# Blocked attention and a gated feed-forward layer on one core: two tiles turned by TensorE instead of by DMA, one product moved, wider products of zeros

## The chip, the cores and the metric

The kernel runs on one core of a Trainium2 chip, in one launch. The metric is the device time of that core in microseconds. A profile of one execution on the chip lies beside the times; its span runs from the first to the last instruction.

## What is computed

Attention within sorted blocks, then a feed-forward layer. `sort_net` is balanced five times (a softmax along rows, then a division along columns) into a matrix P that mixes the eight blocks of k and v; each block of 96 queries attends to its mixed block; the result, laid out by token, goes through `w_in`, `h * cos(h)` and `w_out`:

```python
P = balanced(sort_net)                       # 4 x 8 heads, 8 x 8 blocks, five rounds
k_sorted = einsum('bhij,bhjcd->bhicd', P, k_blocks)
v_sorted = einsum('bhij,bhjcd->bhicd', P, v_blocks)
scores = scale * q_block @ k_sorted_block.T  # 96 x 96 for each block
attn = exp(scores - max); attn = attn / sum(attn)
x = (attn @ v_sorted_block) by token         # 3072 x 512
h = x @ w_in                                 # 512 -> 2048
out = (h * cos(h)) @ w_out                   # 2048 -> 512
```

## The kernel before

The 3072 tokens are worked in eight chunks of 384, numbered n = 0 to 7. A chunk is four token tiles u = 0 to 3 of 96 rows, all eight heads in each. For a tile, `qk(n, u)` (line 490; `qk_half` at 495 does half the heads) makes the scores on TensorE and takes the row maximum off on VectorE; `expo(n, u)` (501) takes the exponential on ScalarE into one of three buffers `p_buf` and has it turned into the tile `pT` (or a piece of `vperm` from chunk 5 on), since the next product needs it turned. The turning goes one of two ways. By default SP issues a DMA transpose (519). With `on_pe`, `p_transpose` (528) does it later: eight TensorE products against the identity into a PSUM tile `pps`, and a copy on the engine that it is given. `av(n, u)` (535) multiplies with the sorted v and divides by the row sum on VectorE, into `xn`; `xn` too must be turned, into `xT[n]`, and again either by a DMA transpose from SP (560) or, with `on_pe`, by `x_transpose` (564): four TensorE products into `xps` and a copy.

The feed-forward layer of a chunk is `moe_up` (633), eight pairs of `up` with the cosine on ScalarE and the product on VectorE, and `moe_down` (638), six groups of `down` (604): group e is half e % 2 of output tile e // 2, eight products of 512 columns each, which add up in one bank of the PSUM pool `acc`. `acc` has two banks, `big` three tiles of two banks. Attention of chunk n + 1 is laid between the groups of chunk n.

The order of all work is written out by hand (`tc.manual_schedule()`, line 67), and each engine works its own queue in that order. Lists of calls stand behind the pieces of `moe_up` and `moe_down`: `slots[e]` runs behind group e, and `mid` inside a group, between its fourth and fifth product. Before the change `mid` is a list that belongs to the last group (line 642). `down` steps through it at line 613.

SP's queue carries the DMA transposes, in the order in which the calls stand, and the stores. GpSimd's queue carries the loads of q, k, v and the weights (line 134 loads a chunk's queries), copies such as `v_permute` (167), and `hold` (521) or `p_hold` (525): a copy of one column that makes GpSimd wait until a tile is there before it goes on.

`keep_warm(times)` (216) issues products of zeros into a tile `idle` of `big` that nobody reads. It is called ahead of the balancing (223), after its first products `sk` (271), and in round 0 of the loop of line 329 (343, three times in that round, none in the others). In each round of the loop ScalarE takes the exponential `E` (331), TensorE sums along the columns (`sk`, 262) and VectorE divides (350, 324, 326), for two groups of batches; the products that turn the first queries (`qps`, 301) stand among them.

The steps of the prediction are these: lines 816 to 834, chunk 1's output with chunk 2's attention; 880 to 882, chunk 4's output with the attention of chunk 5; 895 to 897, chunk 6's output with that of chunk 7.

Of the kernel before, what the change touches and what calls it, by code (L numbers as in the profile page):

```python
# [10 lines left out]
FP32 = mybir.dt.float32  # L11
# [7 lines left out]
def kernel(  # L19
# [15 lines left out]
    nc = tc.nc  # L35
    B, H, S, D = q.shape
# [13 lines left out]
    TC = IC * blk  # L50
# [13 lines left out]
    big = ctx.enter_context(tc.tile_pool(name="big", bufs=3, space=bass.MemoryType.PSUM))  # L64
# [51 lines left out]
    def where(n):  # L116
        b, ih = n // 2, n % 2
        return b // 2, b % 2, ih
# [26 lines left out]
    def q_transpose_dma(n):  # L145
        for e in range(2):
            nc.sync.dma_start_transpose(
                out=q_of(n, e)[:, :QW].rearrange("p (x c) -> p x c", c=blk),
                in_=q_zeroed(n)[:, e * QZ:(e + 1) * QZ])
# [58 lines left out]
    warm = const.tile([128, 128], BF16, name="warm")  # L208
# [6 lines left out]

    def keep_warm(times):

        idle = big.tile([128, 256], FP32, name="idle", tag="big")
        for _ in range(times):
            nc.tensor.matmul(  # L220
                idle[:], warm[:], warm[:, :1].to_broadcast([128, 256]), start=True, stop=True)

    keep_warm(16)


    E_eps = [const.tile([128, nb + 1], FP32, name=f"E{g}") for g in range(NG)]
# [33 lines left out]
    def product(lhs, rhs):  # L260
        ps = acc.tile([128, nb], FP32, name="sk", tag="acc")
        nc.tensor.matmul(  # L262
            ps[:], lhs.rearrange("p x j -> p (x j)"), rhs, start=True, stop=True)
        return ps

    for g in range(NG):
        nc.vector.reciprocal(ci[g][:], cs[g][:])
        nc.vector.scalar_tensor_tensor(
            L[g][:], rows_of, ci[g][:], along(E[g]), op0=ALU.mult, op1=ALU.mult)
    sk = [product(L[g], maskj[:]) for g in range(NG)]  # L270
    keep_warm(3)
    nc.vector.tensor_copy(same[:], rows_of)
    nc.vector.tensor_copy(
        maskp.rearrange("p (b e x) -> p b e x", b=2, e=2),
# [11 lines left out]
    def copy_on(eng, dst, src):  # L286
        if eng is nc.scalar:
            eng.copy(dst, src)  # L288
        else:
            eng.tensor_copy(dst, src)  # L290

    V, A = nc.vector, nc.scalar
# [100 lines left out]
    def k_sort_g(t0, eng, pool, tag):  # L393
        ps = pool.tile([128, 4, 4 * NB], FP32, name="ks", tag=tag)
        for t in range(4):
            k_products(ps, t, t0 + t, slice(0, 128), bds[1].rearrange("p x i -> p (x i)"),
                       pair)
        copy_on(
            eng, kT2[:, ::2, :, :, t0:t0 + 4].rearrange("p e b m t -> p b e m t"),
            ps.rearrange("p t (b e m) -> p b e m t", b=2, e=2))  # L400
# [64 lines left out]
    def v_at(g, b2, hp, h2, i):  # L465
        return (b2 * 2 + hp) * NB + h2 * nb + i
# [34 lines left out]
    def expo(n, u, on_pe=False):  # L501
        p = p_bufs[cnt[0] % NP]
        cnt[0] += 1


        nc.scalar.activation(  # L506
            p[:, :, :blk], s_t.pop((n, u)).rearrange("p e h c -> p (e h) c"), AF.Exp,
            scale=scale)
        if n < LATE:
            t = ptp.tile([128, 2 * H2, blk], BF16, name="pT", tag="pT")  # L510
        else:

            z, w = (n * IC + u) % 8, 2 * H2 * blk
            t = vperm[:, z * w:(z + 1) * w].rearrange("p (a c) -> p a c", c=blk)
        pT[n, u] = t
        if on_pe:
            pb[n, u] = p
        else:
            nc.sync.dma_start_transpose(out=t[:], in_=p.rearrange("p a c -> p (a c)"))

    def hold(t):

        nc.gpsimd.tensor_copy(held[:blk], t[:blk, 0, :1])

    def p_hold(n, u):
        hold(pT[n, u])

    def p_transpose(n, u, eng, pool, tag):
        p = pb.pop((n, u))
        ps = pool.tile([128, 2 * H2, 128], BF16, name="pps", tag=tag)  # L530
        for a in range(2 * H2):
            nc.tensor.transpose(ps[:blk, a, :blk], p[:, a, :blk], ident[:blk, :blk])  # L532
        copy_on(eng, pT[n, u][:blk], ps[:blk, :, :blk])

    def av(n, u, on_pe=False):
        g, b2, ih = where(n)
        if n not in xT:
            xT[n] = xtp.tile([128, KC, TC], BF16, name="xT", tag="xT")
        a = big.tile([128, 2, 512], FP32, name="av", tag="big")
        pt = pT.pop((n, u)).rearrange("p a c -> p (a c)")  # L540
        for hp in range(2):
            for h2 in range(H2):
                e = hp * H2 + h2
                w = 128 if e < 2 * H2 - 1 else blk
                nc.tensor.matmul(  # L545
                    a[:w, hp, h2 * (D + 1):(h2 + 1) * (D + 1)],
                    pt[:blk, e * blk:e * blk + w],
                    vS[g][:, v_at(g, b2, hp, h2, ih * IC + u), :D + 1],
                    start=True, stop=True)
        avv = a[:blk, :, :H2 * (D + 1)].rearrange("p e (h w) -> p e h w", w=D + 1)  # L550
        r = small.tile([blk, 2, H2], FP32, name="r", tag="r")
        nc.vector.reciprocal(r[:].unsqueeze(3), avv[:, :, :, D:])  # L552
        xn = small.tile([blk, H2, 2, D], BF16, name="xn", tag="xn")
        nc.vector.tensor_tensor(  # L554
            xn.rearrange("p h e d -> p e h d"), avv[:, :, :, :D],
            r.to_broadcast([blk, 2, H2, D]), op=ALU.mult)
        if on_pe:
            xn_t[n, u] = xn
        else:
            nc.sync.dma_start_transpose(  # L560
                out=xT[n][:, :, u * blk:(u + 1) * blk],
                in_=xn.rearrange("p h e d -> p (h e d)"))
# [34 lines left out]
    def store(n, ts, o_s, eng=nc.sync):  # L597
        r0 = n * TC + ts * 128
        eng.dma_start(out=out[r0:r0 + 128, :], in_=o_s[:])
# [4 lines left out]
    def down(n, ts, half, stores, mid=()):  # L604
        if half == 0:
            out_ps[ts] = acc.tile([128, Dm], FP32, name="o", tag="acc")
        o = out_ps[ts]
        for f in range(half * FC // 2, (half + 1) * FC // 2):
            nc.tensor.matmul(  # L609
                o[:], gt[n, f // 2][:, f % 2, ts * 128:(ts + 1) * 128], w_out_t[:, f, :],  # L610
                start=(f == 0), stop=(f == FC - 1))
            if f % (FC // 2) == FC // 4 - 1:
                step(mid)
        if half == 0:
            return
        if stores is None:

            z = (n % 2 * 3 + ts) * 2 * Dm
            o_s = vbuf[:, z:z + 2 * Dm].bitcast(FP32)
        else:  # L620
            o_s = op.tile([128, Dm], FP32, name="o_s", tag="o_s")
        late = n > 0 and ts == TC // 128 - 1
        copy_on(V if late else A, o_s[:], o[:])
        if stores is None:
            kept[n, ts] = o_s
        else:
            store(n, ts, o_s, nc.sync if late else stores)

    def step(calls):
        for f, *args in calls:  # L630
            f(*args)
# [3 lines left out]
            up(n, fp, lo, hi)  # L635
            step(slots[fp] if fp < len(slots) else ())

    def moe_down(n, slots=(), stores=nc.sync, mid=()):

        last = 2 * TC // 128 - 1  # L640
        for e in range(last + 1):
            down(n, e // 2, e % 2, stores, mid if e == last else ())
            step(slots[e] if e < len(slots) else ())

    B, C = (big, "big"), (acc, "acc")
# [174 lines left out]
    k_sort_g(8, A, *B)  # L820
    av(2, 0, True)
    k_sort_g(16, A, *B)
    expo(2, 3)
    p_hold(2, 3)
    down(1, 1, 1, nc.sync)
    k_sort_g(12, A, *B)
    av(2, 2, True)
    av(2, 1, True)
    down(1, 2, 0, nc.sync)
    x_transpose(2, 1, V, *B)  # L830
    av(2, 3, True)
# [9 lines left out]
    def ahead(n, *more):  # L841
# [5 lines left out]
        for e, calls in more:  # L847
# [5 lines left out]
    moe_down(2, ahead(3, (0, [(ones, 1)]),  # L853
                      (1, [(w_two,)]), (2, [(p_hold, 3, 3), (load_q, 5), (w_two,)]),
                      (3, [(w_two,)]), (4, [(w_two,)])),
             mid=[(x_transpose, 3, 1, V, *B), (x_transpose, 3, 2, V, *B),
                  (x_transpose, 3, 3, V, *B)])
    q_transpose_dma(5)
    hold(q_turned[1])
    load_q(6)  # L860
# [7 lines left out]
                 [(av, 4, 0)],  # L868
                 [(av, 4, 1, True), (av, 4, 2, True)],
                 [(av, 4, 3, True), (expo, 5, 0), (x_transpose, 4, 1, A, *B, 2), (qk, 5, 1)]],  # L870
             None, mid=[(x_transpose, 4, 3, A, *B)])

    q_transpose_dma(6)
    hold(q_turned[0])
# [2 lines left out]
               [(qk_half, 5, 2, 1)], [], [(qk, 5, 3)]])  # L877
    expo(5, 1)
    expo(5, 2)
    moe_down(4, [[(qk, 6, 0)], [(av, 5, 0), (expo, 5, 3)], [(av, 5, 1), (qk, 6, 1)],  # L880
                 [(av, 5, 2), (expo, 6, 0)], [(av, 5, 3, True), (expo, 6, 1), (qk, 6, 2)]],
             None, mid=[(x_transpose, 5, 3, A, *B)])
    q_transpose_dma(7)
    moe_up(5, [[], [], [(qk_half, 6, 3, 0), (let_go, 4, 0)], [(let_go, 4, 1)], [(let_go, 4, 2)],
               [(qk_half, 6, 3, 1)], [], [(qk, 7, 0)]])
# [1 line left out]
    expo(6, 3)  # L887
    moe_down(5, [[(av, 6, 0)], [(av, 6, 1)], [(av, 6, 2), (qk, 7, 1)],
                 [(av, 6, 3, True), (expo, 7, 0)], [(expo, 7, 1), (qk, 7, 2)]], None,
             mid=[(x_transpose, 6, 3, A, *B)])  # L890
    moe_up(6, [[(let_go, 5, 0)], [(let_go, 5, 1)], [(qk_half, 7, 3, 0), (let_go, 5, 2)], [], [],
               [(qk_half, 7, 3, 1)]])
    expo(7, 2)
    expo(7, 3)
    moe_down(6, [[(av, 7, 0)], [(av, 7, 1)], [(av, 7, 2)], [(av, 7, 3, True)]], None,
             mid=[(x_transpose, 7, 3, A, *B)])
    moe_up(7, [[(let_go, 6, 0)], [(let_go, 6, 1)], [(let_go, 6, 2)]])
    for e in range(2 * TC // 128 - 2):
        down(7, e // 2, e % 2, nc.sync)
# [43 lines left out]
```

## Time and profile before

| What | Value |
|---|---|
| Median of three runs | 245.31 us (244.78 to 245.96) |
| The profiled execution | 245.54 us |
| Its span | 243.8 us |
| Mean granted TensorE clock | 0.949 |
| HBM read, written | 27.27 MB, 6.29 MB |

PE is TensorE's products, PEld its loading of weights, DVE VectorE, ACT ScalarE, POOL GpSimd, SP the queue of SyncE; "SPq" and "POOLq" are the issuing of a transfer. A timeline row reads: start in us, duration in us, engine, line, operation, what is written from what, shape, count, and in brackets how long the engine stood idle ahead of it and what ended that. A row of the chain that ended last reads: start, duration, what. A row of windows reads: from and to, length, busy time of PE, PEld, DVE, ACT and POOL with counts, granted clock (1.00 is full), share of the DMA engines, GB/s. A row of transfers gives the us from issue to landing at its end; a group's row has the shortest, middle and longest duration in ns.

### The profile page before, as it was taken

What the parts mean: (1) busy time and instruction counts of PE and PEld (TensorE: products, weight loads), DVE (VectorE), ACT (ScalarE), POOL (GpSimd) and SP (SyncE); (2) the same over time, 40 slices, a digit from 0 to 9 for tenths busy, and PEclk for the clock granted to TensorE, in tenths of its full rate; (3) what the DMA queues carried; (4) which work ended last, traced back from release to release, by engine and by line L of the source; (5) the groups of instructions that cost most, each with busy time, mean ns of one, the idle gap of its engine ahead of it and who ended that gap; (6) DMA issues with size and microseconds to landing.
All of it is one profiled execution on the core that took longest, in us unless ns stands there. A gap on an engine that the chain in (4) does not pass through costs nothing.

```text
span 243.8 us, 5363 instructions
## 1 busy us (share of the span) xinstructions
PE 230.7 (95%) x2160; PEld 148.4 (61%) x2160; DVE 173.6 (71%) x320; ACT 156.2 (64%) x224; POOL 88.0 (36%) x110
## 2 busy tenths in 40 slices
PE   7979899799999989999999999997999999999994
PEld 5768788565566546656666565654565566446553
DVE  5569678986579955895768987896789769635700
ACT  4468866576488945888569947683568376736611
POOL 6359994099970899010626201700000000000000
PEclk9655599999999999999999999999999999999999
DMA  4999999991999987865789759925581360233012
GB/s 46 231 192 161 184 206 227 198 218 52 166 164 183 162 137 94 128 159 146 120 110 129 77 122 157 182 52 85 117 222 33 89 191 0 53 70 122 1 46 86
DMA packets 67897, 31.20 MB, mean 128 GB/s; under 512 B 56608, under 2 KB 63392, under 8 KB 67616
## 3 DMA queue, kind: packets, MB, share of 16 engines
q0 software_dynamic: 24048, 13.64, 40.6%
q1 hardware_dynamic: 43312, 17.02, 31.2%
q8 instruction: 17, 0.28, 0.5%
q10 hardware_dynamic: 512, 0.20, 0.3%
q14 instruction: 8, 0.07, 0.1%
HBM read 27.27 MB, written 6.29 MB: 138 GB/s over the span
## 4 chain that ended last, share of the span: by engine, by line
PE 77%; DVE 7%; ACT 7%; DMA 6%; issue 1%; ACTq 0%; SPq 0%; DVEq 0%
PE h L585 32%; PE o L609 27%; PE sc L427 3%; PE av L545 3%; PE ks L360 2%; DVE gg L592 2%; PE vs L450 2%; DMA vperm<-p_buf 2%; DMA pT<-p_buf 2%; PE vs L460 2%; DVE xn L554 1%; PE pps L532 1%; PE xps L572 1%; ACT p_buf L506 1%; PE sk L262 1%
## 5 line engine op out<-in xcount | busy, mean ns | idle before, releaser
L585 PE MATMUL h<-xT,w_in_t 128*128 128x384 bf16 (+1 forms) x576 | 92.4, 311 | 1.0 <-DMA xT<-xn 0.5
L609 PE MATMUL o<-w_out_t,gg 128*128 128x512 bf16 x368 | 88.0, 379 | 0.5 <-DVE s L488 0.5
L589 ACT ACTIVATE c<-h,half_pi 128x768 f32<-128x768 f32 (+1 forms) x72 | 59.7, 829 | 28.9 <-PE h L585 26.7
L592 DVE TENSOR_TENSOR gg<-c,h 128x768 bf16<-128x768 f32 (+1 forms) x72 | 61.2, 859 | 22.8 <-ACT c L589 22.7
L585 PEld LDWEIGHTS <-w_in_t 128*128 128x128 bf16 x576 | 53.4, 99 | 28.1 <-issue 1.5
L609 PEld LDWEIGHTS <-gg 128*128 128x128 bf16 x368 | 33.3, 98 | 32.4 <-DVE s L488 0.7
L482 DVE TENSOR_REDUCE mx<-sc 96x4 f32<-96x384 f32 (+1 forms) x43 | 31.9, 742 | 2.9 <-PE sc L427 1.7
L488 DVE TENSOR_TENSOR s<-sc,mx 96x384 f32<-96x384 f32 (+1 forms) x43 | 32.2, 749 | 2.3
L177 POOL COPY vperm<-kv 64x1536 bf16<-64x1536 bf16 (+1 forms) x10 | 27.9, 2826 | 16.1 <-DMA kv<-in_v_dram 16.1
L506 ACT ACTIVATE p_buf<-s 96x768 bf16<-96x768 f32 x32 | 25.9, 839 | 0.6 <-DVE s L488 0.4
L554 DVE TENSOR_TENSOR xn<-av,r 96x512 bf16<-96x512 f32 x32 | 22.0, 687 | 1.1
L552 DVE RECIPROCAL r<-av 96x8 f32<-96x8 f32 x32 | 6.4, 199 | 16.1 <-PE av L545 16.0
L427 PE MATMUL sc<-kTs,q_turned 128*128 128x96 bf16 x224 | 16.1, 206 | 0.7 <-DVE s L488 0.7
L288 ACT CAST kTs<-ks 128x512 bf16<-128x512 f32 (+2 forms) x25 | 12.4, 496 | 6.5 <-PE ks L360 6.4
L134 POOL DMA_DIRECT2D kv<-in_q_dram x24 | 16.0, 683 | 0.8 <-issue 0.6
L427 PEld LDWEIGHTS <-q_turned 128*128 128x128 bf16 x224 | 12.8, 98 | 4.9 <-DVE s L488 1.3
L288 ACT COPY o_s<-o 128x512 f32<-128x512 f32 (+2 forms) x11 | 5.9, 537 | 15.4 <-PE o L609 9.1
L288 ACT COPY kv<-o 128x512 f32<-128x512 f32 x8 | 4.7, 582 | 14.1 <-PE o L609 14.1
L134 POOL DMA_DIRECT2D q_mem<-in_q_dram x16 | 10.6, 677 | 0.6 <-issue 0.6
L589 ACT ACT_TABLE_LOAD x8 | 10.3, 1283 | 0.1
L545 PEld LDWEIGHTS <-pT 96*128 96x128 bf16 (+1 forms) x160 | 7.4, 104 | 4.3 <-ACT pT L288 1.2
L288 ACT CAST pair<-vs 96x512 bf16<-96x512 f32 (+1 forms) x12 | 8.7, 726 | 2.0 <-PE vs L460 2.0
(102 smaller groups left out, 219.1 us busy)
## 6 DMA issues: line engine op xcount, KB each, us to landing
out_dram<-kv SPq DMA_DIRECT2D x12, 256.0 KB, 3.3
out_dram<-o_s SPq DMA_DIRECT2D x11, 256.0 KB, 2.5
w_in_t<-in_moe_w_in_dram POOLq DMA_DIRECT2D x4, 512.0 KB, 11.1
w_out_t<-in_moe_w_out_dram POOLq DMA_DIRECT2D x4, 512.0 KB, 13.7
kv<-in_k_dram POOLq DMA_DIRECT2D x2, 768.0 KB, 13.8
kv<-in_v_dram POOLq DMA_DIRECT2D x2, 768.0 KB, 15.5
pair<-in_k_dram POOLq DMA_DIRECT2D x2, 768.0 KB, 14.0
kv<-in_v_dram POOLq DMA_DIRECT2D x6, 256.0 KB, 8.6
```

The lines of the kernel that those rows point to most:

```text
L134: nc.gpsimd.dma_start(out=q_heads[:, i, :, e], in_=src[:, ih * IC + i, :, e])
L177: nc.gpsimd.tensor_copy(dst, src)
L288: eng.copy(dst, src)
L427: nc.tensor.matmul(out, q_of(n, hp)[:, x:x + 128], keys_of(n, u, h2, hp), start=True, stop=True)
L482: nc.vector.reduce_max(mx[:], scv, axis=AX.X)
L488: nc.vector.tensor_tensor(s, scv, mx.to_broadcast(list(s.shape)), op=ALU.subtract)
L506: nc.scalar.activation(p[:, :, :blk], s_t.pop((n, u)).rearrange("p e h c -> p (e h) c"), AF.Exp, scale=scale)
L554: nc.vector.tensor_tensor(xn.rearrange("p h e d -> p e h d"), avv[:, :, :, :D], r.to_broadcast([blk, 2, H2, D]), op=ALU.mult)
L585: nc.tensor.matmul(h[:, f2, :w], w_in_t[:, kk, f * 128:(f + 1) * 128], xT[n][:, kk, lo:hi], start=(kk == 0), stop=(kk == KC - 1))
L589: nc.scalar.activation(c[:, :, :w], h[:, :, :w], AF.Sin, bias=half_pi[:, 0:1])
L592: nc.vector.tensor_tensor(gt[n, fp][:, :, lo:hi], c[:, :, :w], h[:, :, :w], op=ALU.mult)
L609: nc.tensor.matmul(o[:], gt[n, f // 2][:, f % 2, ts * 128:(ts + 1) * 128], w_out_t[:, f, :], start=(f == 0), stop=(f == FC - 1))
```

## The change

Four edits, all within the hand-written order.

- The last softmax tile of chunk 2 is turned by TensorE and ScalarE instead of by a DMA transpose, into a tile of `acc`, between `av(2, 1)` and the group `down(1, 2, 0)`. GpSimd's hold in front of the next loads waits for tile 2 instead of tile 3.
- `mid` becomes a table from group to calls. Where it was used before it is still for group 5. In chunk 4's output `av(5, 1)` moves out of the slot behind group 2 into the middle of group 3, and so behind `qk(6, 1)`.
- Chunk 7's third token tile is turned by TensorE, behind group 4 of chunk 6's output, with a copy on ScalarE; it had been a DMA transpose.
- The products of zeros have 512 columns instead of 256; sixteen become eight and the first three become two, while round 0 of the balancing keeps its three.

```diff
-        idle = big.tile([128, 256], FP32, name="idle", tag="big")
+        idle = big.tile([128, 512], FP32, name="idle", tag="big")
         for _ in range(times):
             nc.tensor.matmul(
-                idle[:], warm[:], warm[:, :1].to_broadcast([128, 256]), start=True, stop=True)
-
-    keep_warm(16)
+                idle[:], warm[:], warm[:, :1].to_broadcast([128, 512]), start=True, stop=True)
+
+    keep_warm(8)
...
-    keep_warm(3)
+    keep_warm(2)
...
-    def moe_down(n, slots=(), stores=nc.sync, mid=()):
-
-        last = 2 * TC // 128 - 1
-        for e in range(last + 1):
-            down(n, e // 2, e % 2, stores, mid if e == last else ())
+    def moe_down(n, slots=(), stores=nc.sync, mid={}):
+
+        for e in range(2 * TC // 128):
+            down(n, e // 2, e % 2, stores, mid.get(e, ()))
             step(slots[e] if e < len(slots) else ())
...
-    expo(2, 3)
-    p_hold(2, 3)
+    expo(2, 3, True)
+    p_hold(2, 2)
     down(1, 1, 1, nc.sync)
     k_sort_g(12, A, *B)
     av(2, 2, True)
     av(2, 1, True)
+    p_transpose(2, 3, A, *C)
     down(1, 2, 0, nc.sync)
...
-    moe_down(4, [[(qk, 6, 0)], [(av, 5, 0), (expo, 5, 3)], [(av, 5, 1), (qk, 6, 1)],
+    moe_down(4, [[(qk, 6, 0)], [(av, 5, 0), (expo, 5, 3)], [(qk, 6, 1)],
                  [(av, 5, 2), (expo, 6, 0)], [(av, 5, 3, True), (expo, 6, 1), (qk, 6, 2)]],
-             None, mid=[(x_transpose, 5, 3, A, *B)])
+             None, mid={3: [(av, 5, 1)], 5: [(x_transpose, 5, 3, A, *B)]})
...
-    moe_down(6, [[(av, 7, 0)], [(av, 7, 1)], [(av, 7, 2)], [(av, 7, 3, True)]], None,
-             mid=[(x_transpose, 7, 3, A, *B)])
+    moe_down(6, [[(av, 7, 0)], [(av, 7, 1)], [(av, 7, 2, True)], [(av, 7, 3, True)],
+                 [(x_transpose, 7, 2, A, *B)]], None,
+             mid={5: [(x_transpose, 7, 3, A, *B)]})
```

More of the change, by code (lines that the diff above doesn't have):

```diff
@@ L855 @@
                       (3, [(w_two,)]), (4, [(w_two,)])),
-             mid=[(x_transpose, 3, 1, V, *B), (x_transpose, 3, 2, V, *B),
-                  (x_transpose, 3, 3, V, *B)])
+             mid={5: [(x_transpose, 3, 1, V, *B), (x_transpose, 3, 2, V, *B),
+                  (x_transpose, 3, 3, V, *B)]})
     q_transpose_dma(5)
@@ L870 @@
                  [(av, 4, 3, True), (expo, 5, 0), (x_transpose, 4, 1, A, *B, 2), (qk, 5, 1)]],
-             None, mid=[(x_transpose, 4, 3, A, *B)])
+             None, mid={5: [(x_transpose, 4, 3, A, *B)]})
     q_transpose_dma(6)
@@ L889 @@
                  [(av, 6, 3, True), (expo, 7, 0)], [(expo, 7, 1), (qk, 7, 2)]], None,
-             mid=[(x_transpose, 6, 3, A, *B)])
+             mid={5: [(x_transpose, 6, 3, A, *B)]})
     moe_up(6, [[(let_go, 5, 0)], [(let_go, 5, 1)], [(qk_half, 7, 3, 0), (let_go, 5, 2)], [], [],
```

## The prediction

> **What bounds the kernel now.** I read the page first, for the bounding engine and its clock.
>
> ```profile
> PE 230.7 (95%) x2160; PEld 148.4 (61%) x2160; DVE 173.6 (71%) x320; ACT 156.2 (64%) x224; POOL 88.0 (36%) x110
> ...
> PEclk9655599999999999999999999999999999999999
> ...
> PE 77%; DVE 7%; ACT 7%; DMA 6%; issue 1%; ACTq 0%; SPq 0%; DVEq 0%
> ```
>
> TensorE is busy 95% of 243.8 us and makes 77% of the chain that ended last. Time is to be had in two places only: where TensorE stands still behind a transfer (DMA is 6% of the chain), and in slices 2 to 5, where its clock is granted at half. So I next read the timeline of TensorE at each place that the diff touches, then windows of the first 35 us. Starts are used for spacing: a row's span contains the modelled end of its last product, so "idle" understates the time lost.
>
> **Chunk 2's last softmax tile.** The timeline of TensorE, of ScalarE and of GpSimd, the group of tile pT, and, from chunk 1, what turning such a tile on TensorE costs:
>
> ```profile
> 88.60 1.67 PE L609 MATMUL o<-w_out_t,gg 128*128 128x512 bf16 x7
> 90.14 0.34 PE L572 MATMUL xps<-order,xn 96*128 96x96 bf16 x4
> 91.58 0.43 PE L545 MATMUL av<-vS,pT 96*128 96x65 bf16 x8 [1.09 <-DMA pT<-p_buf]
> ```
> ```profile
> 60.15 0.52 PE L532 MATMUL pps<-ident,p_buf 96*96 96x96 bf16 x8
> 60.51 0.38 PE L609 MATMUL o<-w_out_t,gg 128*128 128x512 bf16 x1
> ```
> ```profile
> 87.84 0.58 ACT L288 COPY o_s<-o 128x512 f32<-128x512 f32 x1 [0.35 <-PE o L609]
> 88.33 0.59 ACT L288 CAST kTs<-ks 128x512 bf16<-128x512 f32 x1
> ```
> ```profile
> 91.65 0.18 POOL L523 CAST held<-pT 96x1 f32<-96x1 bf16 x1 [0.18 <-DMA pT<-p_buf]
> ```
> ```profile
> DMA to landing us min/median/max: 2.6/2.6/4.0
> ```
> ```profile
> L288 ACT COPY pT<-pps x7: 784/794/807, 21.8 to 60.9; 96x768 bf16<-96x768 bf16 x7
> ```
> ```profile
> 87.52 4.00 DMA pT<-p_buf
> ```
> ```profile
> 217.75 0.34 PE L572 MATMUL xps<-ident,xn 96*128 96x96 bf16 x4
> 217.92 1.03 PE L609 MATMUL o<-w_out_t,gg 128*128 128x512 bf16 x4
> 219.40 0.32 PE L585 MATMUL h<-xT,w_in_t 128*128 128x384 bf16 x1 [0.45 <-DMA xT<-xn]
> ```
>
> Four xps products take 217.92 - 217.75 = 0.17 us of TensorE, so those at 90.14 are through at 90.31 and av(2,3) starts at 91.58: 1.27 us lost. The transfer took 4.00 us where its kind takes 2.6 in the median; at 2.6 it would have landed at 90.12 and cost nothing. The change removes it from SP's queue and adds eight products, 60.51 - 60.15 = 0.36 us, plus one ScalarE copy of 0.79 us. Before the output group of 88.38 (its second product is the 88.60 of the row), everything the products need is there: p_buf was written when its transfer was issued at 87.52. Their acc bank last held key scores of chunk 1's first output group, and the output group behind them takes the other bank, whose copy o_s ends at 88.42, ahead of 88.38 + 0.36 = 88.74. ScalarE's next copy ends at 88.92; then it copies pT until about 89.75, hidden behind eight output products that end near 90.5. av(2,3) then starts at 90.31 + 0.36 = 90.67: **-0.91 us**. Ends: +0.36 where the transfer would have been punctual or another wait stays, -1.27 if the products vanished in a gap. I take -0.91, as the profiled transfer did come late. The hold on GpSimd moves from tile 3 to tile 2, and gains its 0.18 us of waiting at most, since it starts late anyway; the eight loads of chunk 4's queries behind it are not on the path.
>
> **One product of chunk 5.** Timeline of TensorE, SP's queue, the chain, and the issue's landing time:
>
> ```profile
> 162.82 1.89 PE L609 MATMUL o<-w_out_t,gg 128*128 128x512 bf16 x8
> 166.11 0.43 PE L545 MATMUL av<-pair,vperm 96*128 96x65 bf16 x8 [1.40 <-DMA vperm<-p_buf]
> 166.38 0.51 PE L427 MATMUL sc<-kTs,q_turned 128*128 128x96 bf16 x8
> 166.72 1.89 PE L609 MATMUL o<-w_out_t,gg 128*128 128x512 bf16 x8
> ```
> ```profile
> 161.71 4.36 DMA vperm<-p_buf
> ```
> ```profile
> 166.81 1.23 SPq L519 DMA_TRANSPOSE vperm<-p_buf  x1
> ```
> ```profile
> vperm<-p_buf SPq DMA_TRANSPOSE x1, 2.6
> ```
>
> A group of eight output products takes 1.73 us (spacing 0.216), av(5,1) 0.27 and the scores of chunk 6 0.34, by the starts. The group of 162.82 is through at 164.55, the tile lands at 161.71 + 4.36 = 166.07: 1.56 us lost. After the change the scores (0.34) and four output products (0.86) come first, so TensorE arrives at 165.75 and waits 0.36 us until 166.11. The gain there is 1.20. Next in line is av(5,3): its tile was issued at 166.81 and needed 2.6, so 169.41 to 169.45, on a queue that does not hang on av(5,1). TensorE now arrives at 166.11 + 0.27 + 0.86 + 0.27 + 1.73 = 169.24: 0.2 us come back. **-1.0 us**; ends -1.56 (tile punctual, no wait behind it) and 0 (tiles 2 or 3 as late as tile 1 was). Moving av(5,1) behind the scores puts its two VectorE steps behind theirs; they feed a transfer due only at the next up-projection, 6 us on.
>
> **Chunk 7's third token tile.** TensorE ends chunk 6's output at 217.92 + 4 x 0.216 = 218.78 and starts chunk 7 at 219.40, 0.62 us late, by this transfer, which SP issued only when the two before it were out:
>
> ```profile
> 216.96 2.31 DMA xT<-xn
> ```
> ```profile
> 214.23 2.64 SPq L560 DMA_TRANSPOSE xT<-xn  x1
> ```
> ```profile
> xT<-xn SPq DMA_TRANSPOSE x1, 3.8
> ```
> ```profile
> 218.12 0.48 ACT L288 COPY xT<-xps 128x384 bf16<-128x384 bf16 x1 [2.44 <-PE xps L572]
> ```
>
> It goes; four products (0.17) and one copy (0.48) come, the copy in ScalarE's idle 2.44 us. What is late next: TensorE itself, at 218.95; the fourth tile's copy, 0.17 later, ends at 218.77; tile 1's transfer lands at 214.23 + 3.8 = 218.0. **-0.45 us**; ends -0.62 and +0.17.
>
> **Wider zeros.** TensorE's and ScalarE's timeline, and windows cut where the clock changes:
>
> ```profile
> 6.40 0.49 PE L220 MATMUL idle<-warm 128*128 128x256 bf16 x3
> 7.37 0.35 PE L262 MATMUL sk<-E,same 128*128 128x8 f32 x1 [0.48 <-ACT E L331]
> ```
> ```profile
> 4.03:7.44 3.41, 2.66 (x18) 1.64 (x16) 2.49 (x19) 1.16 (x5) 0.71 (x2) 1.00 1.24 178
> 24.51:27.92 3.41, 2.62 (x32) 2.01 (x31) 3.10 (x10) 2.61 (x5) 3.32 (x4) 0.50 1.18 177
> 27.92:31.33 3.41, 3.41 (x30) 3.24 (x29) 1.40 (x3) 3.09 (x4) 3.34 (x6) 0.50 1.33 193
> 31.33:34.75 3.42, 3.42 (x74) 3.20 (x73) 2.45 (x6) 1.91 (x4) 3.35 (x4) 1.00 1.25 206
> 164.45:167.87 3.42, 2.02 (x24) 1.17 (x23) 1.94 (x4) 0.00 (x0) 0.00 (x0) 1.00 0.71 73
> ```
> ```profile
> 5.45 0.66 ACT L331 ACTIVATE E<-T,ci 128x8 f32<-128x8 f32 x2 [1.16 <-DVE ci L279]
> 7.02 0.30 ACT L331 ACTIVATE E<-T,ci 128x8 f32<-128x8 f32 x1 [0.91 <-DVE ci L326]
> ...
> 10.68 0.30 ACT L331 ACTIVATE E<-T,ci 128x8 f32<-128x8 f32 x1 [0.98 <-DVE ci L326]
> ```
>
> Eight products of 512 columns stream what sixteen of 256 did. The group of three in round 0 doubles: three products of 512 at the 0.216 spacing end about 3 x 0.216 + 0.17 = 0.82 us after 6.40, at 7.22, before the 7.37 at which TensorE waits for ScalarE. The group of two grows by a third and ends before the round's first sk. **0 us** as long as the clock there is full; at half of it the three end near 7.9 and cost 0.5. What the zeros may do to the clock is a rival.
>
> **Sum.** -0.91 - 1.0 - 0.45 = -2.35 us. The profiled run took 245.54 us (span 243.8, 1.7 around it), so 243.2 of its kind; the median of the three runs lies 0.23 below it, at 245.31, which gives 243.0. Between the places TensorE is packed, so a gain is handed on.
>
> **Rivals.** *The clock holds for a window more.* It fell at 7.44 after a window in which much of TensorE's 2.66 us was tiny products, and stays full in a window with 2.02 us, nearly all of it 512 columns wide: what streams counts, and the change adds to that window. Against it: no row shows where the limit lies. If it held to 10.86, a balancing round would take 7.02 - 5.45 = 1.57 us instead of (10.68 - 7.02) / 2 = 1.83: 0.52 in two rounds, about 0.2 more in the last; some is lost again because the window 27.92:31.33 is full at half clock wherever it begins. I take -0.5: **242.5**. The Trainium skill (TensorE: Matmul & The Clock Gate, Part 1) lets the clock fall after an idle window, of about 3.4 us in a free-running grid. The spacing of the edges agrees, 7.44 - 4.03; idleness doesn't, the window had work. By the page's rule alone this rival would not exist, and its grid may lie otherwise in each run.
>
> *Another transfer comes late.* In each stretch with a late tile the trace shows one 16 KB packet of instructions among the transposes:
>
> ```profile
> q8 instruction: 1, 0.02, 5.7%
> ```
>
> (queues, 88.6 to 90.1). A late tile costs 4.36 - 2.6 = 1.8 us. TensorE's stream loses nine of the products of zeros and their weight loads and gets eight transposes with theirs, so behind chunk 2 the fetch comes one product later than before. Hitting tile 2 or 3 of chunk 5, which have 0.2 to 0.7 us to spare, it would cost about 1.5: **244.5**. The Trainium skill (Runtime: NRT & Kernel Launch, Instruction fetch mechanics) gives blocks of 256 instructions and calls the cost mostly hidden; that holds for the engine, the trace shows a transfer beside it paying.
>
> *The grid of the clock falls badly.* If the window that raised the clock at 31.33 stays below the limit, as 24.51:27.92 did, the next one, full at 3.42 us, runs at half: up to 3.4 us, with 0.5 for zeros at half clock. It turns the result from a loss over 2.35 us on: **246.8**. For it: the first 30 us hang together by waits, and a window's content shifts with them. Against it: 27.92:31.33 is packed throughout.
>
> **Chances.** Forecast (242.4 to 243.7) 0.52; clock holds 0.27; another late transfer 0.14; bad grid 0.07. The range 241.9 to 244.7 leaves out the last, and the best of the second. 0.5% is 1.2 us, about what a measurement here can tell: below 244.1 lie the first two cases, 0.79; within, the third, 0.14; above, the fourth, 0.07.
>
> **What would show it.** Right: no wait for pT at av(2,3); at av(5,1) under 0.5 us; chunk 7's h starts with the last output product. Wrong: a new wait behind TensorE's pps or at av(5,2), av(5,3); a tile over 4 us elsewhere; another fall or rise of the clock than at 7.44 and 31.33.

## The result and the profile after

The changed kernel takes 243.17 us in the median of 19 runs, the kernel before 245.17 us in 19 beside it; the ratio is 0.9946 with a 95% interval of 0.9922 to 0.997. A second measurement (e10 below) gives 0.9936 (0.9908 to 0.9965). The ratio compares means and leaves out one disturbed execution of the changed kernel, at 252.56 us; by it the change is worth 1.3 us (0.7 to 1.9), while the medians lie 2.0 us apart.

The profiled execution took 244.09 us with a span of 242.3. The chain that ended last has lost half of its transfers. The list of TensorE's waits began with two transfers in the kernel before and now has none among its first entries. The chain's shares after, the first two waits before, the first four after:

```profile
PE 83%; ACT 7%; DVE 4%; DMA 3%; issue 1%; ACTq 0%; DVEq 0%
```
```profile
PE av L545 <- DMA vperm<-p_buf: 1.4, 1, 1.4
PE av L545 <- DMA pT<-p_buf: 1.1, 1, 1.1
```
```profile
PE idle L220 <- DVE warm L209: 1.0, 1, 1.0
PE ks L360 <- DVE kTs L290: 0.8, 1, 0.8
PE sc L427 <- DVE s L488: 0.7, 1, 0.7
PE xps L572 <- DVE xn L554: 0.5, 2, 0.3
```

The timeline of TensorE at the three places, first chunk 2, then chunk 5, then chunk 7:

```profile
89.34 0.54 PE L532 MATMUL pps<-ident,p_buf 96*96 96x96 bf16 x8
89.71 1.89 PE L609 MATMUL o<-w_out_t,gg 128*128 128x512 bf16 x8
91.44 0.34 PE L572 MATMUL xps<-order,xn 96*128 96x96 bf16 x4
91.61 0.42 PE L545 MATMUL av<-vS,pT 96*128 96x65 bf16 x8
```
```profile
164.93 1.03 PE L609 MATMUL o<-w_out_t,gg 128*128 128x512 bf16 x4
165.79 0.42 PE L545 MATMUL av<-pair,vperm 96*128 96x65 bf16 x8
166.05 1.03 PE L609 MATMUL o<-w_out_t,gg 128*128 128x512 bf16 x4
166.91 0.42 PE L545 MATMUL av<-pair,vperm 96*128 96x65 bf16 x8
167.17 1.89 PE L609 MATMUL o<-w_out_t,gg 128*128 128x512 bf16 x8
169.13 0.43 PE L545 MATMUL av<-pair,vperm 96*128 96x65 bf16 x8
```
```profile
216.72 0.34 PE L572 MATMUL xps<-ident,xn 96*128 96x96 bf16 x4
216.89 1.03 PE L609 MATMUL o<-w_out_t,gg 128*128 128x512 bf16 x4
217.75 1.46 PE L585 MATMUL h<-xT,w_in_t 128*128 128x384 bf16 x8
```

Each start follows the one ahead of it by that row's own products (0.17 us for four transposes, 0.86 for four output products, 1.73 for eight), but for 169.13: there av(5,3) waits about 0.23 us.

To compare executions I use stretches between starts of first products: S2 from chunk 1's output to chunk 2's up-projection, S5 from chunk 4's output to chunk 5's, S7 from chunk 6's output to chunk 7's. T0 is the start of chunk 0's first output product. S2 went from 15.60 to 14.68 us, S5 from 14.16 to 12.91, S7 from 12.40 to 11.97: 2.60 us less in the three. But T0 went from 47.90 to 48.85: this execution did not see a full clock until 33.66. The page prints 1.00 ahead of that because it has no record there; the products of zeros tell, 634 ns in the median for 512 columns, where an execution with a full clock from 3.77 on (e10) has 482 in the median and 376 at the shortest.

```profile
L220 PE MATMUL idle<-warm x13: 587/634/634, 1.0 to 7.6; 128*128 128x512 bf16 x13
```

The stretch from chunk 7's up-projection to the end went from 24.37 to 24.53 us; the same work ends at the same distance, and the last store and the closing waits behind it take longer. The three stretches, T0 and this end together make the 1.5 us by which the span fell.

A stretch needs the record of its first product. The traces of e1 to e8 lack 21 of 400 records of output products, the first of chunk 4 and of chunk 6 among them: the first group shows seven records over 1.51 us there, where the other traces show eight over 1.73. So one product's spacing, 0.22 us, is added to S5 and S7 in these eight rows of the table below. Where an expectation rests on S5 or S7 of one of these kernels, its value is 0.22 us lower.

### The profile page after: what moved, and what is told of

It reads as the page before. It is cut to its first block, busy times and chain, and to the rows that moved or that the text cites. A ratio compares the mean times of both kernels' runs of the same rounds, so it can differ in the third digit from the quotient of the medians.

```text
span 242.3 us, 5366 instructions
## 1 busy us (share of the span) xinstructions
PE 232.8 (96%) x2163; PEld 149.2 (62%) x2163; DVE 173.7 (72%) x320; ACT 157.6 (65%) x226; POOL 88.2 (36%) x110
## 4 chain that ended last, share of the span: by engine, by line
PE 83%; ACT 7%; DVE 4%; DMA 3%; issue 1%; ACTq 0%; DVEq 0%
PE h L585 33%; PE o L609 28%; PE sc L427 4%; PE av L545 3%; PE ks L360 3%; PE idle L220 2%; DMA vperm<-p_buf 2%; ACT p_buf L506 2%; PE xps L572 2%; PE sk L262 2%; PE vs L460 2%; DVE gg L592 1%; PE vs L450 1%; ACT kTs L288 1%; ACT vS L288 1%; PE pps L532 1%
## 5 line engine op out<-in xcount | busy, mean ns | idle before, releaser
L288 ACT COPY xT<-xps 128x384 bf16<-128x384 bf16 (+1 forms) x9 | 4.6, 513 | 8.1 <-PE xps L572 8.1
```

## The experiments

Theory M was the prediction's: each edit acts at its place. Its rival, F, came from comparing the two traces: the tile of av(5,1), which landed 4.36 us after its issue before, took 2.9 us after, so av(5,1) was moved away from a wait that was no longer there. (Some expectations call it the first tile of chunk 5; it is the second, as tile 0 is issued already in chunk 3's output.) F says a transposing transfer is late only when a 16 KB packet of instructions for TensorE falls among its packets, and that a small shift of the stream or of the run moves the packet. All stretches, from one profiled execution each (* with 0.22 us added):

| Kernel | T0 | clock full first | full again at | S2 | S5 | S7 | median us | ratio to before (95%) |
|---|---|---|---|---|---|---|---|---|
| before | 47.90 | 4.03 to 7.44 | 31.34 | 15.60 | 14.16 | 12.40 | 245.17 | |
| after | 48.85 | none | 33.66 | 14.68 | 12.91 | 11.97 | 243.17 | 0.9946 (0.9922 to 0.997) |
| e1 | 48.07 | 4.91 to 8.33 | 32.22 | 14.67 | 12.83* | 11.82* | 243.41 | 0.9909 (0.9885 to 0.9932) |
| e2 | 47.84 | none | 30.93 | 16.09 | 12.92* | 11.81* | 244.34 | 0.9954 (0.9931 to 0.9977) |
| e3 | 48.37 | 6.03 to 9.44 | 33.33 | 15.69 | 13.98* | 11.83* | 245.48 | 1.0009 (0.998 to 1.0038) |
| e4 | 49.00 | none | 33.65 | 14.67 | 14.13* | 11.98* | 244.36 | 0.9961 (0.9928 to 0.9993) |
| e5 | 49.10 | none | 33.88 | 14.67 | 12.93* | 11.82* | 242.93 | 0.9933 (0.9904 to 0.9962) |
| e6 | 48.15 | 5.54 to 8.96 | 32.85 | 15.85 | 12.83* | 11.88* | 245.09 | 0.9997 (0.9964 to 1.003) |
| e7 | 48.29 | none | 32.25 | 14.67 | 13.40* | 11.79* | 244.54 | 0.9974 (0.9936 to 1.0011) |
| e8 (before again) | 47.85 | 4.63 to 8.04 | 31.94 | 15.93 | 12.88* | 11.80* | one run | |
| e9 | 47.95 | 5.24 to 8.66 | 32.55 | 14.67 | 12.91 | 11.80 | 243.11 | 0.9912 (0.9888 to 0.9937) |
| e10 (after again) | 47.72 | 3.77 to 10.59 | 31.07 | 14.67 | 12.91 | 11.95 | 243.52 | 0.9936 (0.9908 to 0.9965) |
| e11 | 47.58 | 3.84 to 10.66 | 31.14 | 14.67 | 12.91 | 11.90 | 243.24 | 0.9924 (0.989 to 0.9957) |
| e12 (e5 again) | 47.60 | 3.87 to 10.69 | 31.17 | 14.67 | 12.91 | 11.78 | 242.90 | 0.993 (0.9899 to 0.9961) |

**e1: chunk 2's tile alone.**

```diff
-    expo(2, 3)
-    p_hold(2, 3)
+    expo(2, 3, True)
+    p_hold(2, 2)
...
+    p_transpose(2, 3, A, *C)
```

> The kernel before with only chunk 2's last softmax tile turned by TensorE. Stretches are measured between first products: chunk 1's output to chunk 2's up-projection took 15.60 us before and 14.68 after; chunk 4's output to chunk 5's up-projection 14.16 and 12.91. Theory F (a tile is late only where a 16 KB packet of instructions falls among its transfer's packets, and any change to TensorE's stream ahead of it can move that packet): 14.7 for the first stretch, and 12.6 to 13.0 for the second if the packet near 163.7 us moves off the first tile of chunk 5, though nothing of chunk 5 is changed. Theory M (the edits do it, each at its own place): 14.7 and 14.2. In all about 0.9 us less than before by M, about 2.2 by F.

This one edit gives, in four runs, no less than the whole change: 0.9909. S2 fell as in the full change, and S5 to 12.83, as low as the changed kernel's, though nothing of chunk 5 was edited. The timeline of TensorE has av(5,1) in its old slot, right behind its group of eight, with no wait:

```profile
162.07 1.89 PE L609 MATMUL o<-w_out_t,gg 128*128 128x512 bf16 x8
163.80 0.42 PE L545 MATMUL av<-pair,vperm 96*128 96x65 bf16 x8
164.06 0.51 PE L427 MATMUL sc<-kTs,q_turned 128*128 128x96 bf16 x8
```

M falls for chunk 5, and for chunk 7 (11.82 with its third tile on DMA). That this edit moved the packets is not shown by it: the kernel before does as well in its second profile (e8).

**e2: av(5,1) moved, alone.**

```diff
-            down(n, e // 2, e % 2, stores, mid if e == last else ())
+            down(n, e // 2, e % 2, stores, mid if e == last else mids.get(e, ()))
...
-    moe_down(4, [[(qk, 6, 0)], [(av, 5, 0), (expo, 5, 3)], [(av, 5, 1), (qk, 6, 1)],
+    moe_down(4, [[(qk, 6, 0)], [(av, 5, 0), (expo, 5, 3)], [(qk, 6, 1)],
...
-             None, mid=[(x_transpose, 5, 3, A, *B)])
+             None, mid=[(x_transpose, 5, 3, A, *B)], mids={3: [(av, 5, 1)]})
```

> The kernel before with only av(5,1) moved into the middle of group 3; TensorE gets the same number of instructions. Both theories leave the packet at its place and chunk 2's stretch at 15.6 us. M, by the prediction's own sum: chunk 5's stretch 13.2 us (14.16 less 1.0), 0.36 us of waiting left at av(5,1) and 0.2 at av(5,3). F says the same as long as the packet still meets the first tile; if it meets the second, 12.7 to 13.2.

S5 was 12.92, not the 13.2 that both theories gave while the packet met the tile of av(5,1). It didn't: it began 0.03 us ahead of the tile's issue, at 162.1, and the transfer took 2.59. The same number of instructions, and yet another place of the packet: F's count of instructions is too simple. S2 stayed long, at 16.09, and its last tile took 4.49 us. The runs do show a gain, 0.9954 with an interval below 1.

**e3: the zeros alone.**

```diff
-        idle = big.tile([128, 256], FP32, name="idle", tag="big")
+        idle = big.tile([128, 512], FP32, name="idle", tag="big")
...
-    keep_warm(16)
+    keep_warm(8)
...
-    keep_warm(3)
+    keep_warm(2)
```

> The kernel before with only the products of zeros changed: nine products and nine loads of weights fewer in TensorE's stream ahead of everything. M: chunk 2's stretch 15.6 us and chunk 5's 14.2, time as before to 0.3 us. F: the packets move; if the one near 88.7 us moves off chunk 2's last tile that stretch is 14.3 us, 1.3 less without any edit of attention; the same at chunk 5, 12.6 to 13.0. The clock, if the wider zeros hold it a window longer: back at full at 31.3 but with the first fall at 10.9 instead of 7.4, 0.5 us less.

No gain: 1.0009. A packet came 1.90 us after the issue of chunk 2's last tile and another 1.91 us after that of av(5,1)'s, so both were late still; F's hope that nine products fewer would clear them was wrong.

**e4: the change with av(5,1) back.**

```diff
-    moe_down(4, [[(qk, 6, 0)], [(av, 5, 0), (expo, 5, 3)], [(qk, 6, 1)],
+    moe_down(4, [[(qk, 6, 0)], [(av, 5, 0), (expo, 5, 3)], [(av, 5, 1), (qk, 6, 1)],
...
-             None, mid={3: [(av, 5, 1)], 5: [(x_transpose, 5, 3, A, *B)]})
+             None, mid={5: [(x_transpose, 5, 3, A, *B)]})
```

> The changed kernel with av(5,1) back in its old slot behind group 2. M: chunk 5's stretch goes back up by 1.0 to 1.25 us, from 12.91 to about 14.1. F: its tile's transfer took 2.9 us in the changed kernel, not 4.4, so the old slot would wait 0.1 us only and the stretch stays at 12.9 to 13.1.

M's number came: S5 14.13, 1.2 us more than in the changed kernel, and the wait is back.

```profile
162.99 1.89 PE L609 MATMUL o<-w_out_t,gg 128*128 128x512 bf16 x8
166.25 0.43 PE L545 MATMUL av<-pair,vperm 96*128 96x65 bf16 x8 [1.36 <-DMA vperm<-p_buf]
```

The tile took 4.32 us and the packet began 2.23 us behind its issue. In all kernels with av(5,1) moved (after, e2, e5, e9 to e12) the packet began between 0.03 us ahead of the issue and 0.57 behind it, and the tile took 2.5 to 3.2 us. In the seven with it in the old slot the tile was late in three (before, e3, e4: packet 1.9 to 2.2 us behind) and punctual in four; in two of these, e1 and e8, the packet began 0.1 us ahead of the issue. So the move may help by taking the packet off the tile, but seven profiles against seven do not settle that, nor do the runs, 0.9961 against 0.9946 with intervals that overlap. How it would is open: the packet of e4 began at 164.11, before TensorE came to av(5,1) at 162.99 + 1.73 = 164.72, so the wait there did not place it.

**e5 and e12: the change with chunk 7's third tile on DMA.**

```diff
-    moe_down(6, [[(av, 7, 0)], [(av, 7, 1)], [(av, 7, 2, True)], [(av, 7, 3, True)],
-                 [(x_transpose, 7, 2, A, *B)]], None,
+    moe_down(6, [[(av, 7, 0)], [(av, 7, 1)], [(av, 7, 2)], [(av, 7, 3, True)]], None,
```

> The changed kernel with chunk 7's third token tile turned by a DMA transpose again. The stretch from chunk 6's first output product to chunk 7's first up product took 12.40 us before and 11.97 after. M (the edit is what gained there): 12.4 us, the whole 0.4 us slower. F (it was late only because a packet of instructions held up the first of the three transfers): 11.6 us where the third is issued by about 215.5 or earlier, 0.3 us less than with the edit; up to 12.4 where the packet still holds up the first.

> The changed kernel with chunk 7's tile on DMA, once more, beside the changed kernel on one chip. F: 0.2 to 0.4 us faster than the changed kernel, stretch of chunk 7 11.6 us. M: 0.4 us slower, 12.4.

S7 was 11.82 and 11.78, where the kernels with the edit have 11.97 (after), 11.98 (e4) and 11.95 (e10). With the tile on DMA, chunk 7's up-projection still follows the last four output products by 0.87 us, without a wait (e12):

```profile
215.44 1.03 PE L609 MATMUL o<-w_out_t,gg 128*128 128x512 bf16 x4
216.31 1.95 PE L585 MATMUL h<-xT,w_in_t 128*128 128x384 bf16 x11
```

So the edit costs its four products, 0.17 us, where the transfers are punctual. The last stretch, from chunk 7's up-projection to the end, is also longer with it: 24.53 or 24.54 us in after, e4 and e10, 24.36 to 24.38 in all others but e7. Medians of 242.93 and 242.90 stand against 243.17 and 243.52 with the edit; the intervals of the ratios overlap, so the runs alone do not settle 0.2 us.

**e6: zeros in products of 128 columns.**

```diff
-    keep_warm(16)
+    keep_warm(32)
...
-    keep_warm(3)
+    keep_warm(6)
```

(and 128 for 256 in `keep_warm`, 6 for 3 in round 0)

> The kernel before with the same columns of zeros in products of 128: 22 products and 22 loads of weights more in TensorE's stream, nothing else changed. F: the packets fall some 2 to 5 us earlier against the work; chunk 2's stretch goes from 15.60 to 14.33 us if neither of its last two tiles is met, and chunk 5's from 14.16 to 12.7: up to 2.7 us less without an edit of attention. M: 15.6 and 14.2, time as before.

As before, 0.9997. The packet left chunk 2's last tile and met the third instead, 1.9 us behind its issue, which took 4.2 us; av(2,2) and av(2,1) waited, and av(2,3) did not:

```profile
89.61 0.68 PE L545 MATMUL av<-vS,pT 96*128 96x65 bf16 x16 [1.33 <-DMA pT<-p_buf]
...
92.08 0.42 PE L545 MATMUL av<-vS,pT 96*128 96x65 bf16 x8
```

**e7: no zeros.** The three calls of `keep_warm` are left out.

```diff
-    keep_warm(16)
...
-    keep_warm(3)
...
-        keep_warm(3 if it == 0 else 0)
```

> The kernel before without any products of zeros (none is read by anything): 22 products and their loads fewer. F: the packets fall 2 to 5 us later; chunk 2's stretch 14.3 us, chunk 5's anything from 12.6 to 14.2 by where the packet falls. M: 15.6 and 14.2. The clock, if the zeros are what raises it early: no full window before about 31 us in any run, and the time to chunk 0's first output product (47.9 us before) longer by 0.3 to 1.0 us; if an early full window is worth nothing, 47.9 or less.

The packet fell at 92.1, behind everything, and chunk 2's last tile was there in time by DMA:

```profile
90.87 0.34 PE L569 MATMUL xps<-order,xn 96*128 96x96 bf16 x4
91.05 0.42 PE L542 MATMUL av<-vS,pT 96*128 96x65 bf16 x8
```

S2 came to 14.67, not 14.3. Another packet, 0.08 us behind the issue of chunk 2's first tile, goes with 3.51 us for that tile; the third was then issued 3.69 us behind the first (e8: 3.27) and landed at 88.53 after its usual 2.61, and the av products that start at 88.58 waited for it. The stretch from chunk 7's up-projection to the end was over a microsecond longer than in the others (25.68 us; 24.37 before), with the last packet, at 239.5, among the final stores. No run had an early full window, as expected (mean clocks 0.994 to 1.0), and T0 was 48.29, within what kernels with zeros show; the time is 0.9974 (0.9936 to 1.0011) of before. The zeros bought nothing that these runs can show.

**e8: the kernel before once more.** Nothing is edited.

> The kernel before once more, for a second profile of the same stream. If the packets' places are set by the stream alone: chunk 2's stretch 15.6 us, chunk 5's 14.2, chunk 7's 12.4, as in the first profile. If they move from run to run: one or more of them without the late tile, at 14.3, 12.7 or 11.6.

The same program had S5 12.88 and S7 11.80 this time, as good as any variant; chunk 2's last tile was late again (S2 15.93). The timeline of TensorE, chunk 2 and chunk 5:

```profile
90.10 0.34 PE L572 MATMUL xps<-order,xn 96*128 96x96 bf16 x4
91.87 0.43 PE L545 MATMUL av<-vS,pT 96*128 96x65 bf16 x8 [1.43 <-DMA pT<-p_buf]
```
```profile
163.11 1.89 PE L609 MATMUL o<-w_out_t,gg 128*128 128x512 bf16 x8
164.84 0.42 PE L545 MATMUL av<-pair,vperm 96*128 96x65 bf16 x8
165.10 0.51 PE L427 MATMUL sc<-kTs,q_turned 128*128 128x96 bf16 x8
```

In the first profile a packet began at 163.67, 1.96 us behind the issue of av(5,1)'s tile. Here the transfers' view, 161.8 to 162.05 us, has it 0.1 us ahead of the issue, and the tile on time:

```profile
q8 instruction: 1, 0.02, 21.9%
issues: line engine op xcount, KB each, median us to landing
vperm<-p_buf SPq DMA_TRANSPOSE x1, 2.6
```

So the packets also move from run to run.

**e9: two edits.** e1's and e2's edits together.

```diff
-    expo(2, 3)
-    p_hold(2, 3)
+    expo(2, 3, True)
+    p_hold(2, 2)
...
+    p_transpose(2, 3, A, *C)
...
-    moe_down(4, [[(qk, 6, 0)], [(av, 5, 0), (expo, 5, 3)], [(av, 5, 1), (qk, 6, 1)],
+    moe_down(4, [[(qk, 6, 0)], [(av, 5, 0), (expo, 5, 3)], [(qk, 6, 1)],
...
-             None, mid=[(x_transpose, 5, 3, A, *B)])
+             None, mid=[(x_transpose, 5, 3, A, *B)], mids={3: [(av, 5, 1)]})
```

> The kernel before with two of the four edits: chunk 2's tile turned by TensorE and av(5,1) moved; zeros and chunk 7 as before. F: the chunk 7 edit costs 0.2 to 0.4 us where the three transfers follow each other undisturbed, and the zeros do little, so this is 0.2 us faster than the changed kernel run beside it, with stretches of 14.7, 12.7 and 11.6 us. M: 0.4 us slower than the changed kernel, 12.4 in the last.

**e10: the change again**, nothing edited, on the same chip.

> The changed kernel once more on the same chip as its variants, for comparison and for a second profile. Both theories: 243.0 to 243.4 us in most runs; stretches 14.7, 12.7 to 12.9, and 11.8 to 12.0 us. Runs without a full clock before 31 us about 1 us longer.

e9 is 0.9912 and e10 0.9936: F's sign, with intervals that overlap; M's 0.4 us slower did not come. S5 was 12.91 in both, as in e2; the packet, 0 to 0.2 us behind the issue of av(5,1)'s tile, did not delay it enough to matter (2.54 and 3.07 us).

**e11: more zeros.** e12 with one product more in each of rounds 1 to 3.

```diff
-        keep_warm(3 if it == 0 else 0)
+        keep_warm(3 if it == 0 else 1)
```

> The changed kernel with chunk 7's tile on DMA again and one more product of zeros (512 columns) in each of rounds 1 to 3 of the balancing. If what streams through TensorE decides, more runs keep the full clock for a second window of 3.4 us: mean granted clocks of 0.955 to 0.958 in most runs that warm up early, instead of about one in four, and those 0.4 to 0.8 us shorter. If streaming doesn't decide, clocks as in the same kernel without the three products, and up to 0.5 us longer, as each stands in front of a step of the balancing.

Six of its 12 runs kept the full clock for two windows (mean clock 0.955 to 0.957). Of the kernels with zeros of 512 columns and no more of them (after, e3, e4, e5, e10, e12) 14 of 67 runs did; of the 86 runs with the old zeros whose clock is listed, and of e6's ten, none. Among the runs with any early full window (mean clock under 0.98) it is six of eight against 14 of 52. So more columns of zeros go with a longer early full clock. That streamed columns are what decides is not shown: in e11's own profile the added products start at 8.67, 10.26 and 12.04, behind the window that held the clock (3.84 to 7.25, six products of 512 columns, 3072); the window behind it, with two of them and 24 products of 96 columns, has 3328, and the clock fell at its end. Between these kernels it is worth little: 0.9924 against e12's 0.993. Windows of e10, which kept the clock from 3.77 to 10.59, and the end of the balancing on VectorE before, then in e10:

```profile
3.77:7.18 3.41, 3.14 (x16) 1.38 (x13) 2.50 (x20) 1.34 (x6) 0.91 (x2) 1.00 1.21 167
7.18:10.59 3.41, 2.63 (x34) 2.15 (x34) 2.24 (x19) 1.27 (x5) 2.43 (x4) 1.00 1.10 231
10.59:14.01 3.42, 2.95 (x54) 2.49 (x54) 2.19 (x9) 2.24 (x5) 0.19 (x1) 0.50 0.91 188
```
```profile
12.56 0.35 DVE L282 SCALAR_TENSOR_TENSOR bd<-maskp,ci,T 128x128 bf16<-128x128 f32 x1
```
```profile
11.80 0.35 DVE L282 SCALAR_TENSOR_TENSOR bd<-maskp,ci,T 128x128 bf16<-128x128 f32 x1
```

The balancing ends 0.76 us sooner, and T0 only 0.18 (47.72 against 47.90).

**The packets over all profiles.** From the trace records of the 14 profiles: 479 transposing transfers of softmax and token tiles, 56 of them over 3.8 us. Each of the 56 has a packet of instructions that begins 0.9 to 2.2 us behind its issue, and of all transfers with such a packet only four were not that late. Of the 382 without a packet between 0.3 us ahead of the issue and 2.6 us behind it, none was that late (3.64 us at most). This counts what happens together; by what means the packet holds the transfer up was not looked at.

## Why the prediction was right, and where not

The total was right: 243.0 forecast, 243.17 measured, faster as forecast. In part that is luck: two of its three gains stand against a profile in which two transfers happened to be late, and by the ratio the change gives 1.3 us where the sum has 2.35. Its steps:

- **Chunk 2** was right in mechanism and size: 0.91 forecast, 0.92 in the profiles, and in the four profiles of kernels with that tile on DMA and zeros of 256 or 512 columns (before, e2, e3, e8) it was late, with S2 of 15.60 to 16.09 us. Its end of +0.36, for a punctual transfer, did not occur in these four; with narrow zeros (e6) and with none (e7) the tile was punctual, 2.64 and 2.58 us. By itself the edit gives 0.9909 (e1).
- **Chunk 5** failed as a step, though its sum (1.0, measured 1.25) looks right. The prediction let the tile land at 166.07 as before, hid a part of the wait and left 0.36 us at av(5,1). In the profile the tile was punctual and no wait remained; only the 0.2 us at av(5,3) came as forecast. The step that failed is the tacit one that the late tile is a fixed cost of the place: in the kernel before it was late in one of two profiles (14.16, 12.88), and with av(5,1) in the old slot in three of seven, with it moved in none of seven. Whether the move does that or chance stays open. By itself the move gives 0.9954 (e2), but beside chunk 2's edit nothing more (e9 0.9912, e1 0.9909), and bringing it back in e4 costs 1.2 us of S5 in one profile.
- **Chunk 7** gave 0.43 against 0.45 in these two profiles, and again by chance: the kernel before without its late transfer has 11.80 (e8), and there the edit costs 0.17 us, and 0.16 more at the end of the kernel. The prediction had +0.17 as an end; that end is the usual case: of the eleven profiles with this tile on DMA ten have S7 between 11.78 and 11.90, one 12.40.
- **Zeros** cost nothing, as forecast (e3: 1.0009).
- **The rival of the clock** is real: 14 of 67 runs. One reading behind it was too strong: of the 24 products in the window 164.45:167.87 eight have 512 columns, the others 96 and 65. Its price of 0.5 stays open. In the profile of e10 the 0.7 us in the balancing was right (0.76), but almost all of it is gone by chunk 0's output. Of the changed kernel's first 18 undisturbed runs the four with two early full windows have a median of 242.72 us, the ten with one 243.16: 0.4 less. In e5 and e12 they are no shorter. Where the time goes was not tried.
- **The rival of the late transfer** had the right cause, a packet of instructions, and the wrong time: it was put down as a danger of the change, and stands beside each late tile, those of the waits at chunk 2 and chunk 5 among them. Ahead of the wait at chunk 7 too a packet stood beside a late tile (its first token tile, 4.33 us, packet 1.27 us behind the issue), and the third was issued behind that one, 4.02 us after the first. A late first tile alone does not make the wait: in e8 it took 4.24 us with a packet 1.86 us behind, the third was issued 3.32 us after it, and landed in time.
- **The rival of the bad grid** came in the profiled run, without an early full window and full only at 33.66. It cost 0.95 us at T0, not 3.8; the four runs without an early window have a median of 244.59 us, 1.4 above the ten with one. The prediction priced a whole window at double time; that VectorE and ScalarE set much of the pace there (3.10 and 2.61 of 3.41 us busy in its row 24.51:27.92) fits the smaller cost, and was not tested.

## What to carry to other kernels

A wait in one profile is one draw: profile the same kernel twice before an edit is aimed at it, and look at what else was on the queues in the late case. A route around a transfer costs its own instructions in every run, so what it is worth hangs on how often the transfer is late: chunk 2's tile was late in four of six profiles on DMA and the route took 0.92 us off; chunk 7's wait came in one of eleven, and in the other ten the route would only cost its 0.17. And test edits that came together one by one: here one of four gives, in four runs, as much by itself as all of them.

## What the runs showed of the hardware

- A transposing transfer is longer where a 16 KB packet of instructions falls beside it. Without one it took 2.6 us (softmax tiles) or 2.3 us (token tiles) in the median. With one that begins 0.9 to 2.2 us behind its issue it took 1.7 us more in the median; with one between 0.3 us ahead and 0.9 us behind, 0.8 us more in the median of 27 and 1.4 at most; with one later than that, up to 2.6 us behind, under 0.1 us more (ten transfers). The Trainium skill (Runtime: NRT & Kernel Launch, Instruction fetch mechanics) has the fetch in blocks of 256 instructions as mostly hidden; the profiles agree with the size, about 17 packets for some 4300 instructions of TensorE, and the cost is paid by the transfer beside it.
- The granted clock changes at edges that lie whole multiples of 3.41 us apart (4.03, 7.44 and 31.34 in the kernel before) and whose place differs from run to run. The window 4.03 to 7.44, in which seven products of zeros of 256 columns and nine products of 8 columns start, let the clock fall, and none of the 86 runs with the old zeros kept it full for two windows; e10's window 3.77 to 7.18, with six of 512 columns and eight of 8, held it. How much must stream, and whether columns are the measure, was not settled.
